# Windowed attention and a top-1 expert layer on one core: two transposing blocks and two couples of pieces a step in place of four single ones

## The chip, the cores and the metric

The kernel runs on one core of a Trainium2 chip. The metric is the device time in microseconds (us) of one execution; of several runs the median is given. A profile is one further execution, recorded by the hardware profiler, with its own time. The engines are named as in the profile: PE (TensorE matmuls; PEld are its weight loads), DVE (VectorE), ACT (ScalarE), POOL (GpSimd) and SP (the queue from which most transfers are issued).

## What is computed

Eight batches of eight heads, 576 rows of 64 columns each, go through causal attention in which a row sees itself and the 63 rows before it. The eight heads side by side make 4608 rows x of 512 columns, and each row goes through one of eight experts.

```
    scores = scale * np.matmul(q, k.transpose(0, 1, 3, 2))
    mask = (rel >= 0) & (rel < window)
...
    attn = np.exp(scores)
    attn = attn / (np.sum(attn, axis=-1, keepdims=True) + 1e-09)
    return np.matmul(attn, v).astype(np.float32)
...
    logits = x @ w_gate + modality_bias[modality_id]
    e_idx = np.argmax(logits, axis=1)
...
        h = np.maximum(x[mask] @ w1[e], 0.0)
        out[mask] = gate_w[mask, None] * (h @ w2[e])
```

w1 is 512 x 1024 and w2 1024 x 512 for each expert. The gate weight is the router's probability of the chosen expert. Everything is float32.

## The kernel before, in words

**Two streams of work.** The 576 rows of a batch are cut into blocks of 64; 72 blocks make 36 pairs (`NPR`). The loop at line 1023 has steps s = 0 to 39, and each step carries several pairs at several stages of attention: the scores of pair s, the probabilities of pair s - 1, the values of pair s - 2, the router's logits of pair s - 3. A group is two pairs, and there are 18 groups (`NG`). In odd steps the rows of group R = (s - 5) // 2 get their ranks within their experts (`route2`, `counts`, `route3`, lines 734 to 796) and are then scattered by POOL into a scratch tensor in HBM that is sorted by expert. From step 12 on (`FIRST`), the expert layer's work on rows that lie there already is mixed into the same steps.

**Slots and pieces.** A slot is 256 rows of one expert. Its products are split into a high and a low part (three float32r matmuls for one product) and dealt out in 16 pieces by a generator, `slot_pieces` (line 268); each call of `gap(it, True)` (line 462) puts the next piece on PE. `first` (line 292) is 12 matmuls of 256 columns into the bank `em`; two of them make 256 columns of the hidden layer, which ACT (`hh`, line 312) and DVE (`hl`, line 313) then copy out. `second` (line 316) is 6 matmuls of 512 columns into `y0` or `y1`, which DVE scales (line 334) and POOL scatters to the output (line 337). What a piece leaves for the other engines is kept in `later` and issued at the next `run_later()`. From step 13 on there are four pieces in a step: in three steps of four, two of `first` and then two of `second`; in the fourth (16, 20, 24 and so on) `second`, `first`, `first`, `second`.

**What a step of attention puts on PE.** `values` (32 small matmuls, line 668), `logits` (line 697), `scores` (line 612), then `probs_t` twice: four transposes of 128 x 128 into a bank, which ACT copies to `pT` (line 647). Below, p0 and p1 are these two groups of four. Then exps on ACT (line 638, eight a pair, in parts of two, three and three), `x_t` (four transposes of the attention's rows, copied by ACT to `xaT`, line 689, which the next step's logits read), and, up to step 33, two parts of `heads_t` (line 566): four transposes each of loaded q or k rows of group G = s // 2 + 1, copied to `kT` or `qT` by `heads_out` (line 575). Even steps take k (`PARTS[0]`: K0, K1), odd steps q. The copies are DVE's, except K1's, which is ACT's.

**Banks.** All these transposes, the logits and the ranks write to PSUM banks of 512 float32 a partition, which `turn_bank` (line 514) hands out. Up to step 11 it takes turns among five banks. From step 13 on it hands out the two banks `tp` of `ps_t` alone (line 474), and who asks for a bank waits until its last reader is through.

**What sets the order.** The order on every engine is that of the program (line 869, `manual_schedule`). PE, ACT and DVE each work through their queue in that order. Small DVE work that isn't urgent is queued: `routing` holds the steps of `route1` and `route3` (the largest logit, the one-hot row `oh`, its running sum, the target row, the scatter), `queue` the planner's. `tick(n)` (line 129) issues n of them, routing's first. `weights(s)` (line 1011) splits loaded weights into their two parts, on ACT and DVE. `plan` (line 804), at the end of a step, takes the counts of a group and queues what decides the next slot's rows. SP issues all loads in the order of the program: q, k and v at the head of a step, weights in `weights`, a slot's rows in `fetch`.

**A step from 13 on, before the change, by the order on PE:** values, logits, scores, p0, p1; piece 1; x_t; piece 2; the first part of the heads; the ranks (odd steps); piece 3; the second part of the heads; piece 4.

Of the kernel before, what the change touches and what calls it, by code (L numbers as in the profile page):

```python
# [26 lines left out]
def tile_window_attn_moe(  # L27
# [12 lines left out]
    nc = tc.nc  # L40
# [10 lines left out]
    NPR = NBLK // 2  # L51
    GB = 2
    GBLK = 2 * GB
    NG = NPR // GB
# [9 lines left out]
    EARLY = ((2, (0, 1)), (4, (0, 1)), (6, (0, 1)), (8, (0, 1)), (9, (1, 2)), (10, (1, 2)), (11, (1, 2)),  # L64
             (12, (0, 2)), (13, (0, 2)), (15, (0, 2)))
    WEIGHTS = 5
    FIRST = 12
# [16 lines left out]
    tab = ctx.enter_context(tc.tile_pool(name="tab", bufs=1))  # L84
# [44 lines left out]
    def tick(n=1, table=False):  # L129
        for _ in range(n):  # L130
            if routing and not table:
                routing.pop(0)()
            elif queue:
                queue.pop(0)()
                issued[0] += 1
# [111 lines left out]
    def run_later():  # L247
        while later:
            later.pop(0)()
# [207 lines left out]
    def counted():  # L457
        for _ in slot_pieces():
            position[0] += 1
            yield  # L460

    def gap(it, wait=False):

        if next(it, "end") != "end" and not wait:
            run_later()
            tick()

    def turn(out_, in_, p0=0):
        n = in_.shape[0]
        nc.tensor.transpose(out=out_, in_=in_, identity=ident[p0:p0 + n, p0:p0 + n])  # L470
# [10 lines left out]
    pl = actx.enter_context(tc.tile_pool(name="pl", bufs=2))  # L481
# [11 lines left out]
    def by_group(x):  # L493
        return x.rearrange("p (a h j) i -> p a h j i", a=2, h=HP)
# [19 lines left out]
    def turn_bank(s):  # L514

        i = n_tp[0]
        n_tp[0] += 1
        if s < FIRST and i % 5 > 1:
            return ps_m.tile([P, 512], F32, name=("em", "y0", "y1")[i % 5 - 2])
        return ps_t.tile([P, 512], F32, name="tp")  # L520
# [13 lines left out]
    def swap_v(p):  # L534

        nc.gpsimd.tensor_copy(out=ve[p][0:W64], in_=vo[p][0:W64])
# [29 lines left out]
    def heads_t(G, nm, i, tp):  # L566


        src = qk[G, nm].rearrange("p t (h a) d -> p t h (a d)", a=2)
        for h in range(2):  # L570
            for t in range(2):
                n = 2 * h + t
                turn(tp[:, n * P:(n + 1) * P], src[:, t, 2 * i + h])

    def heads_out(tp, G, nm, i, copy):
        dst = by_group(qT if nm == "q" else kT)[:, G % 2, 2 * i:2 * i + 2]
        copy(out=dst.rearrange("p h j (i t) -> p h t (j i)", t=2),
             in_=tp.rearrange("p (h t i) -> p h t i", h=2, t=2))
# [54 lines left out]
    def exps(p, us):  # L633
        ss, mn, sm = st[p, "s"]
        for u in us:
            a, hp = divmod(u, HP)
            h = 2 * hp + a
            nc.scalar.activation(  # L638
                out=ss[a][:, hp, :], in_=ss[a][:, hp, :], func=AF.Exp,
                bias=mn[:, h:h + 1], scale=-1.0, accum_out=sm[:, h:h + 1])  # L640
# [43 lines left out]
    def x_t(p, xp):  # L684
        xa = st[p, "xa"]
        for c in range(NC1):
            turn(xp[:, c * P:(c + 1) * P], xa[:, c * P:(c + 1) * P])
        xaT = st[p, "xT"] = work.tile([P, DM], F32, name="xaT")
        nc.scalar.copy(out=xaT, in_=xp)
# [44 lines left out]
    def route2(G, tp):  # L734

        while routing:
            routing.pop(0)()
        oh = chosen[G]
        rk = tp[:, 0:GB * E]
        nc.tensor.matmul(  # L740
            out=rk, lhsT=tri, rhs=oh[:, 1:].rearrange("p j e -> p (j e)"), start=True, stop=False)
        for j in range(GB):
            sh = [P, GB - j, E]
            nc.tensor.matmul(
                out=rk[:, j * E:], lhsT=ones, rhs=oh[:, j:j + 1, :].broadcast_to(sh),
                start=False, stop=(j == GB - 1))
        return rk
# [43 lines left out]
    def counts(G, tp):  # L791
        cp = tp[:, GB * E:E + GB * E]
        nc.tensor.matmul(out=cp, lhsT=ones, rhs=chosen[G + 1][:, 0, :], start=True, stop=True)
        return cp

    def counts_out(pool, cp):
        cnt = pool.tile([1, E], F32, name="cnt")
        nc.vector.tensor_copy(out=cnt, in_=cp[0:1])
        return cnt
# [68 lines left out]
    it = counted()  # L868
# [142 lines left out]
    def weights(s):  # L1011

        if halves:
            split_lo(*halves.pop(0))
        if len(raws) == 2 or raws and not pieces:
            split_hi(*raws[0])
            halves.append(raws.pop(0))
        while pieces and len(raws) < 2:
            x, c = pieces.pop(0)
            raw = epool.tile([P, WCH], F32, name="y", bufs=4)  # L1020
            raws.append((load_piece(raw, evs[x], c), x, c))

    for s in range(NPR + 4):
        j = s % GB
        for f, args in at.pop(s, ()):
            f(*args)
        n_tick = 6 if s < FIRST else 5
        n_gap = 0 if s < FIRST else 4
        G = s // GB + 1
        heads = PARTS[j] if G < NG else ()  # L1030
        R = (s - 5) // GB if s >= 5 and j == 1 else -1
        if 1 <= s < FIRST:
            swap_upper(s - 1)

        if 2 <= s < NPR + 2:
            values(s - 2)
            if s <= FIRST:
                values_out(s - 2)
        if 3 <= s < NPR + 3:
            logits(s - 3, turn_bank(s) if s != FIRST else ps_m.tile([P, 512], F32, name="y0"))  # L1040
            if (s - 3) % GB == GB - 1:
                route1((s - 3) // GB)
        if FIRST < s < NPR + 2:
            values_out(s - 2)
        if s < NPR:
            scores(s)
            if s == FIRST:
                x_turn(fetched[0])
                gap(it, True)
            minima(s)  # L1050
            if s == FIRST - 2:
                tick(todo[0][-1] - issued[0], table=True)
        if 1 <= s <= NPR:
            if s == FIRST:
                run_later()
            if s >= FIRST:
                swap_upper(s - 1)
            swap_v(s - 1)
            for a in range(2):
                probs_t(s - 1, a, turn_bank(s))  # L1060
            sums(s - 1)
        if s < NPR:
            exps(s, (0, 1))
        if s == 0:
            first_pair(1, (both[:1], both[1:]))
            cast_bias()
        if n_gap > 0 and s != FIRST:
            gap(it, True)
        if 2 <= s < NPR + 2:
            x_t(s - 2, turn_bank(s) if s != FIRST else ps_m.tile([P, 512], F32, name="y0"))  # L1070
        run_later()
        tick(2)
        if s < NPR:
            exps(s, (2, 3, 4))
        if n_gap > 0:
            if FIRST < s < FIRST + 4 or s % 2:
                weights(s)
            if s != FIRST:
                gap(it, True)
        if heads:  # L1080
            tp = turn_bank(s)
            heads_t(G, *heads[0], tp)
            heads_out(tp, G, *heads[0], nc.vector.tensor_copy)
        if s == FIRST:
            weights(s)
            gap(it, True)
        run_later()
        tick(n_tick)
        cnt = None
        if R >= 0:  # L1090
            tp = turn_bank(s)
            rk = route2(R, tp)
            if R == NG - 1 or any(R == T for T, _ in EARLY):
                cnt = counts_out(tab if R == NG - 1 else pl, counts(R, tp))
            route3(R, rk)
        if s < NPR:
            exps(s, (5, 6, 7))
        if n_gap > 2:
            if FIRST <= s < FIRST + 4:
                weights(s)  # L1100
            gap(it, True)
        if heads:
            tp = turn_bank(s)
            heads_t(G, *heads[1], tp)
            heads_out(tp, G, *heads[1], nc.scalar.copy if heads[1] == K1 else nc.vector.tensor_copy)
        run_later()
        tick(n_tick)
        if s == WEIGHTS:
            load_weights()
        if s >= WEIGHTS:  # L1110
            weights(s)
        if n_gap > 3:
            gap(it, True)
        run_later()
        if s == 1:
            select_bias()
        if s == 4:
            nc.sync.dma_start(out=xs_blk[DUMMY:DUMMY + 2].rearrange("b p c -> p b c"), in_=padrow)
        for T, xs_ in EARLY:
            if T == R:  # L1120
                plan(T, xs_, cnt)
# [20 lines left out]
    tab = Room()  # L1142
# [99 lines left out]
    while next(it, "end") != "end":  # L1242
# [6 lines left out]
        for n in range(RAWS):  # L1249
            if n < len(swaps) and n == len(ahead) and swaps[n][0] <= t + RAWS:  # L1250
                _, buf, x, c = swaps[n]
# [18 lines left out]
    with tc.If(trip > 0):  # L1270
        NS = N // P + E
        with ExitStack() as gctx:
# [38 lines left out]
            with tc.For_i(0, trip, 1) as it:  # L1311
# [25 lines left out]
                for n in range(F // 512):  # L1337
                    tp = gps.tile([P, 512], F32, name="gxp")
# [53 lines left out]
```

## Time and profile before

| | |
|---|---|
| median of 3 runs | 622.42 us (621.82 to 624.05) |
| the profiled execution | 621.29 us |
| its span, from the first to the last instruction | 619.6 us |
| PE busy | 603.5 us (97%), 6365 matmuls |
| PE weight loads | 542.2 us (88%) |
| DVE busy | 381.8 us (62%), 1486 instructions |
| ACT busy | 297.4 us (48%), 933 instructions |
| POOL busy | 139.7 us (23%), 315 instructions |
| mean granted TensorE clock | 0.992 |
| from HBM and to HBM | 67.49 MB and 23.91 MB |

A row of the timeline reads: start and length in us, the engine, the line of the kernel, the operation, output <- inputs by the program's names, shapes, and how many alike were merged into the row; in brackets how long the engine stood idle before it and who released it. A row of a group of instructions gives, after the bar, the busy time in us and the mean of one in ns, and after a second bar the idle time ahead of them. Matmuls overlap, and their ends are modelled, so their spacing is read from one start to the next. Step 14 begins at 95.13 us, step 16 at 116.21, step 18 at 138.23, step 19 at 148.71, and step 33 ends at 307.15, by the first `values` matmul of a step.

### The profile page before, as it was taken

Reading aid. Unit: us, or ns where it says so; the run is one execution under the profiler, and the core shown is the slowest. Engines: PE = TensorE matmul, PEld = TensorE weight load, DVE = VectorE, ACT = ScalarE, POOL = GpSimd, SP = SyncE. Lnnn points to the kernel's source line nnn. Section 1 sums busy time; section 2 is a strip of 40 time slices with the busy share of each in tenths; the row PEclk is TensorE's granted clock in tenths of the full one; section 3 lists DMA queues with packets and bytes.
Section 4 is the critical chain, followed back from the end, with each engine's and each line's share of the span. In section 5 each row is a group of like instructions: output and inputs, shape, how many; then the busy total and the mean of one; then the engine's idle time right before and its main releaser. Section 6 shows DMA issues by size and latency. Waiting matters only on the chain. (4 is left out here: it accounts for less than half of the span.)

```text
span 619.6 us, 17314 instructions
## 1 busy us (share of the span) xinstructions
PE 603.5 (97%) x6365; PEld 542.2 (88%) x6365; DVE 381.8 (62%) x1486; ACT 297.4 (48%) x933; POOL 139.7 (23%) x315
## 2 busy tenths in 40 slices
PE   8999889999999999999999999999999999999996
PEld 5888778889898998989898899999999989999986
DVE  3899987877776877667656465323324734776622
ACT  3999886765757555636463111111112513554411
POOL 6333422042313320321223131011001101102202
PEclk7999999999999999999999999999999999999999
DMA  9999865764675754463313034522243534678300
GB/s 163 216 234 246 204 183 166 188 188 126 167 205 123 194 135 99 137 155 84 107 54 103 35 103 167 174 69 69 51 155 116 167 126 137 203 239 249 108 18 21
DMA packets 158983, 88.08 MB, mean 142 GB/s; under 512 B 122618, under 2 KB 141616, under 8 KB 158768
## 3 DMA queue, kind: packets, MB, share of 16 engines
q1 hardware_dynamic: 150272, 67.45, 43.1%
q0 software_dynamic: 5888, 18.93, 8.1%
q8 instruction: 51, 0.84, 0.6%
q10 hardware_dynamic: 2736, 0.58, 0.5%
q14 instruction: 36, 0.29, 0.2%
HBM read 67.49 MB, written 23.91 MB: 148 GB/s over the span
## 5 line engine op out<-in xcount | busy, mean ns | idle before, releaser
L326 PE MATMUL y<-Whi,hh 128*128 128x512 f32 x288 | 116.9, 406 | 0.0
L638 ACT ACTIVATE ss<-ss,mn 128x128 f32<-128x128 f32 x288 | 112.6, 398 | 4.0 <-DMA wg<-in_moe_w_gate_dram 3.3
L326 PE MATMUL y<-Wlo,hh 128*128 128x512 f32 x288 | 112.7, 391 | 0.0
L326 PE MATMUL y<-Whi,hl 128*128 128x512 f32 x288 | 112.5, 391 | 0.0
L337 POOL DMA_INDIRECT out_dram<-y,id x36 | 39.8, 1107 | 232.7 <-DVE y L334 159.9
L313 DVE SCALAR_TENSOR_TENSOR hl<-em,hh 128x512 fp32r<-128x512 f32 x50 | 34.5, 690 | 92.8 <-ACT hh L312 82.1
L304 PE MATMUL em<-xh,Whi 128*128 128x256 f32 x400 | 83.7, 290 | 0.0
L312 ACT ACTIVATE hh<-em 128x512 fp32r<-128x512 f32 x50 | 29.6, 592 | 105.2 <-PE em L304 86.9
L304 PE MATMUL em<-xl,Whi 128*128 128x256 f32 x400 | 79.3, 280 | 0.0
L304 PE MATMUL em<-xh,Wlo 128*128 128x256 f32 x400 | 79.1, 279 | 0.0
L647 ACT COPY pT<-tp 128x512 f32<-128x512 f32 x57 | 31.4, 589 | 70.2 <-PE tp L470 60.9
L626 DVE CUSTOM_DVE_ANT_0 ss<-sp,masks 128x128 f32<-128x128 f32 x288 | 63.5, 286 | 2.4 <-PE sp L612 2.3
L326 PEld LDWEIGHTS y<-Whi,hl 128*128 128x128 f32 x288 | 54.1, 188 | 12.2
L304 PEld LDWEIGHTS em<-xh,Whi 128*128 128x128 f32 x400 | 62.3, 189 | 1.8
L326 PEld LDWEIGHTS y<-Whi,hh 128*128 128x128 f32 x288 | 54.2, 188 | 8.2
L326 PEld LDWEIGHTS y<-Wlo,hh 128*128 128x128 f32 x288 | 54.2, 188 | 7.9
L304 PEld LDWEIGHTS em<-xl,Whi 128*128 128x128 f32 x400 | 60.9, 188 | 0.0
L304 PEld LDWEIGHTS em<-xh,Wlo 128*128 128x128 f32 x400 | 60.9, 188 | 0.0
L638 ACT ACTIVATION_READ_ACCUMULATOR ss<-ss,mn 128x1 f32 x288 | 56.0, 195 | 0.0
L773 POOL DMA_INDIRECT xs_scratch<-xa,idx x36 | 36.4, 1012 | 81.8 <-DVE lm L716 40.3
L312 ACT ACTIVATE hh<-sp 128x512 fp32r<-128x512 f32 x22 | 13.2, 598 | 75.9 <-PE sp L304 73.9
L668 PEld LDWEIGHTS av<-ve,pT 128*64 128x64 f32 x576 | 36.3, 138 | 13.2 <-issue 8.2
(240 smaller groups left out, 1211.3 us busy)
## 6 DMA issues: line engine op xcount, KB each, us to landing
xt<-xs_scratch SPq DMA_DIRECT2D x72, 128.0 KB
vo<-in_v_dram SPq DMA_DIRECT2D x32, 256.0 KB
y<-in_moe_w_dram SPq DMA_DIRECT2D x32, 256.0 KB
vo<-in_moe_w_dram SPq DMA_DIRECT2D x24, 256.0 KB
ss<-in_moe_w_dram SPq DMA_DIRECT2D x24, 256.0 KB
xs_scratch<-xs_scratch SPq DMA_DIRECT2D x8, 514.0 KB
pT<-in_moe_w_dram SPq DMA_DIRECT2D x16, 256.0 KB
qk<-in_k_dram SPq DMA_DIRECT2D x14, 256.0 KB
```

What stands on the lines that cost most here:

```text
L304: nc.tensor.matmul(out=hb[:, i * TP:(i + 1) * TP], lhsT=w[buf][:, c0:c0 + P], rhs=x[:, c * TP:(c + 1) * TP], start=(n == 0), stop=(n == le ...
L312: nc.scalar.activation(out=hh, in_=hb, func=AF.Relu),
L313: nc.vector.scalar_tensor_tensor(out=hl, in0=hb, scalar=0.0, in1=hh.bitcast(F32), op0=ALU.max, op1=ALU.subtract)))
L326: nc.tensor.matmul(out=sl["y", t], lhsT=h[:, i * TP + t * P:i * TP + (t + 1) * P], rhs=w[buf][:, c0:c0 + DM], start=(k == 0 and n == 0), s ...
L337: ins = nc.gpsimd.indirect_dma_start(out=out, out_offset=bass.IndirectOffsetOnAxis(ap=sl["id"][:, t:t + 1], axis=0), in_=y, in_offset=None ...
L626: nc.vector.tensor_tensor_reduce(out=ss[a][:, hp, :], in0=sp[a][:, hp * P:(hp + 1) * P], in1=mask, scale=-1.0 / 8.0, scalar=3.0e38, op0=AL ...
L638: nc.scalar.activation(out=ss[a][:, hp, :], in_=ss[a][:, hp, :], func=AF.Exp, bias=mn[:, h:h + 1], scale=-1.0, accum_out=sm[:, h:h + 1])
L647: nc.scalar.copy(out=pT, in_=pp)
L668: nc.tensor.matmul(out=by_block(av)[c * W64:(c + 1) * W64, a, :, hp, :], lhsT=pT[:, i:i + W64], rhs=(vo if c else ve)[p][:, 2 * hp + a, :] ...
L773: ins = nc.gpsimd.indirect_dma_start(out=xs, out_offset=bass.IndirectOffsetOnAxis(ap=idx[:, j:j + 1], axis=0), in_=xg[j], in_offset=None)
```

## The change

From step 13 on, the transposing work of a step stands in two blocks in place of four. The ranks of an odd step are put at its very beginning, ahead of `values`. The first part of the heads follows the probabilities, ahead of piece 1. Pieces 1 and 2 follow each other, with the evictions of piece 1, three ticks, three exps and `weights` issued between them. `x_t` and the second part of the heads follow piece 2, then two ticks, five ticks, the last three exps, and pieces 3 and 4. The exps 2 to 4 stay behind piece 1; the exps 5 to 7 stay ahead of piece 3, now behind the copies of x_t and of the second part. `plan` stays at the end of the step. Up to step 12 the order is as it was. The order on PE from step 13 on becomes: ranks (odd steps), values, logits, scores, p0, p1, first part of the heads; pieces 1 and 2; x_t, second part of the heads; pieces 3 and 4.

The diff:

```diff
@@ -1029,6 +1029,26 @@
         G = s // GB + 1
         heads = PARTS[j] if G < NG else ()
         R = (s - 5) // GB if s >= 5 and j == 1 else -1
+
+        def part(i):
+            if not heads:
+                return
+            tp = turn_bank(s)
+            heads_t(G, *heads[i], tp)
+            heads_out(tp, G, *heads[i], nc.scalar.copy if heads[i] == K1 else nc.vector.tensor_copy)
+
+        def ranks():
+            tp = turn_bank(s)
+            rk = route2(R, tp)
+            n = None
+            if R == NG - 1 or any(R == T for T, _ in EARLY):
+                n = counts_out(tab if R == NG - 1 else pl, counts(R, tp))
+            route3(R, rk)
+            return n
+
+        cnt = None
+        if s > FIRST and R >= 0:
+            cnt = ranks()
         if 1 <= s < FIRST:
             swap_upper(s - 1)
 
@@ -1064,45 +1084,41 @@
         if s == 0:
             first_pair(1, (both[:1], both[1:]))
             cast_bias()
-        if n_gap > 0 and s != FIRST:
+        if s > FIRST:
+            part(0)
+            gap(it, True)
+            run_later()
+            tick(3)
+            if s < NPR:
+                exps(s, (2, 3, 4))
+            if s < FIRST + 4 or s % 2:
+                weights(s)
             gap(it, True)
         if 2 <= s < NPR + 2:
             x_t(s - 2, turn_bank(s) if s != FIRST else ps_m.tile([P, 512], F32, name="y0"))
+        if s > FIRST:
+            part(1)
         run_later()
         tick(2)
-        if s < NPR:
+        if s < NPR and s <= FIRST:
             exps(s, (2, 3, 4))
-        if n_gap > 0:
-            if FIRST < s < FIRST + 4 or s % 2:
-                weights(s)
-            if s != FIRST:
-                gap(it, True)
-        if heads:
-            tp = turn_bank(s)
-            heads_t(G, *heads[0], tp)
-            heads_out(tp, G, *heads[0], nc.vector.tensor_copy)
+        if s <= FIRST:
+            part(0)
         if s == FIRST:
             weights(s)
             gap(it, True)
         run_later()
         tick(n_tick)
-        cnt = None
-        if R >= 0:
-            tp = turn_bank(s)
-            rk = route2(R, tp)
-            if R == NG - 1 or any(R == T for T, _ in EARLY):
-                cnt = counts_out(tab if R == NG - 1 else pl, counts(R, tp))
-            route3(R, rk)
+        if s <= FIRST and R >= 0:
+            cnt = ranks()
         if s < NPR:
             exps(s, (5, 6, 7))
         if n_gap > 2:
             if FIRST <= s < FIRST + 4:
                 weights(s)
             gap(it, True)
-        if heads:
-            tp = turn_bank(s)
-            heads_t(G, *heads[1], tp)
-            heads_out(tp, G, *heads[1], nc.scalar.copy if heads[1] == K1 else nc.vector.tensor_copy)
+        if s <= FIRST:
+            part(1)
         run_later()
         tick(n_tick)
         if s == WEIGHTS:
```

## The prediction

> **What bounds the kernel now.** I read the page first, then the waits of TensorE, then the busy time by step, then the timeline of single steps.
>
> ```profile
> span 619.6 us, 17314 instructions
> ...
> PE 603.5 (97%) x6365; PEld 542.2 (88%) x6365; DVE 381.8 (62%) x1486; ACT 297.4 (48%) x933; POOL 139.7 (23%) x315
> ...
> PEclk7999999999999999999999999999999999999999
> ...
> L647 ACT COPY pT<-tp 128x512 f32<-128x512 f32 x57 | 31.4, 589 | 70.2 <-PE tp L470 60.9
> ```
>
> PE is busy 97% of the span. A busy PE could still hide stretched matmuls, so I cut the stage that the change touches at the first `values` matmul of each step.
>
> ```profile
> core 0: us, PE busy (x) PEld busy (x) DVE busy (x) ACT busy (x) POOL busy (x), PEclk, DMA share, GB/s
> 0.00:20.00 20.00, 17.13 (x184) 12.47 (x188) 10.29 (x65) 9.57 (x35) 10.09 (x54) 0.83 0.90 169
> ...
> 116.21:127.57 11.36, 10.68 (x138) 9.41 (x137) 8.73 (x40) 7.78 (x26) 2.63 (x5) 1.00 0.59 162
> ...
> 138.23:148.71 10.48, 10.48 (x138) 9.45 (x137) 6.85 (x35) 5.45 (x22) 2.87 (x4) 1.00 0.54 151
> 148.71:159.33 10.62, 10.62 (x141) 9.59 (x140) 7.86 (x32) 7.61 (x25) 1.98 (x6) 1.00 0.69 167
> 95.13:307.15 212.02, 211.34 (x2758) 190.38 (x2757) 154.16 (x715) 128.07 (x450) 54.76 (x110) 1.00 0.58 151
> ```
>
> 95.13 to 307.15 holds steps 14 to 33. PE is idle for 0.68 us of it, all in step 16 (116.21 to 127.57); the other steps follow each other without a hole. So nothing runs beside PE that could absorb a delay: a stop of PE there moves the end by its own length, and the only gain to be had is in PE's own spacing, or in step 16's stop.
>
> **The new order on PE.** Before: front (values, logits, scores, eight transposes of probabilities), piece, x_t, piece, heads[0], ranks, piece, heads[1], piece. After: ranks, front, heads[0], two pieces, x_t, heads[1], two pieces. Ranks and each transposed part hold a `tp` bank of `ps_t`, of which there are two, and from step 13 on nothing else is drawn from. Before, a piece (about 1.4 us) stood ahead of x_t and heads[0], in which the earlier bank was emptied. After, three groups of four transposes (p0, p1 of the probabilities, then heads[0]) stand back to back on two banks: one of them must wait for ACT to copy out p0. The trace shows this wait once, in step 16, and what it consists of:
>
> ```profile
> 118.74 0.65 PE L470 MATMUL tp<-ident_r,ss 128*128 128x128 f32 x4
> ...
> 119.44 0.59 ACT L647 COPY pT<-tp 128x512 f32<-128x512 f32 x1
> ...
> 120.08 0.66 PE L470 MATMUL tp<-ident_r,ss 128*128 128x128 f32 x4 [0.68 <-ACT pT L647]
> ...
> 120.49 0.48 PE L326 MATMUL y<-Whi,hh 128*128 128x512 f32 x1
> ```
>
> p1 waits there for ACT's copy of p0: copy ends 119.44 + 0.59 = 120.03, PE resumes at 120.08, 0.05 later. Now the undisturbed pace, from three groups on different banks, and the copies of an even step (18), an odd one (19), step 13 and one late case (29):
>
> ```profile
> 26.36 0.66 PE L470 MATMUL em<-ident_r,ss 128*128 128x128 f32 x4
> 26.86 0.60 PE L470 MATMUL y<-ident_r,ss 128*128 128x128 f32 x4
> 27.29 0.60 PE L470 MATMUL y<-ident_r,xa 128*128 128x128 f32 x4
> ...
> 140.76 1.09 PE L470 MATMUL tp<-ident_r,ss 128*128 128x128 f32 x8
> ...
> 141.46 1.07 ACT L647 COPY pT<-tp 128x512 f32<-128x512 f32 x2 [3.90 <-PE tp L470]
> ...
> 151.24 1.09 PE L470 MATMUL tp<-ident_r,ss 128*128 128x128 f32 x8
> ...
> 151.99 1.08 ACT L647 COPY pT<-tp 128x512 f32<-128x512 f32 x2 [2.26 <-PE tp L470]
> ...
> 86.38 0.66 PE L470 MATMUL tp<-ident_r,ss 128*128 128x128 f32 x4
> ...
> 87.44 0.66 PE L470 MATMUL tp<-ident_r,ss 128*128 128x128 f32 x4 [0.41 <-DVE lg L702]
> ...
> 256.82 1.09 PE L470 MATMUL tp<-ident_r,ss 128*128 128x128 f32 x8
> ...
> 258.13 0.59 ACT L647 COPY pT<-tp 128x512 f32<-128x512 f32 x1 [3.75 <-PE tp L470]
> ```
>
> A third group is ready 27.29 - 26.36 = 0.93 us after p0 begins. In an even step ACT's copy of p0 begins 0.70 after p0 and takes 0.589, so the bank is free to PE at 0.70 + 0.59 + 0.05 = 1.34: PE stops 0.41. The first group after a stop takes 0.50 (26.36 to 26.86), a following one 0.43: another 0.07. Together 0.48. In an odd step the copy begins 0.75 after p0: 0.53. ACT cannot begin earlier, since it starts as soon as p0 has landed. Behind the waiting transposes stand both pieces of the first couple, and nothing of PE can pass them.
>
> heads[0] exists in steps 13 to 33, 21 steps. In step 13 p1 is already held up to 1.06 after p0 by DVE's logits, so heads[0] would come at 1.06 + 0.50 = 1.56, after p0's bank is free. In step 16 p1 sits in p0's bank, and heads[0] finds the other one empty. Both keep their old stops and get no new one. The rest: 10 odd x 0.53 + 9 even x 0.48 = **+9.6 us**.
>
> **What the joining saves.** Step 18 before and rows in which a couple runs unbroken:
>
> ```profile
> 141.61 0.48 PE L304 MATMUL em<-xh,Whi 128*128 128x256 f32 x2
> ...
> 143.12 0.60 PE L470 MATMUL tp<-ident_r,xa 128*128 128x128 f32 x4
> 143.47 0.48 PE L304 MATMUL em<-xh,Whi 128*128 128x256 f32 x2
> ...
> 330.86 0.37 PE L304 MATMUL em<-xh,Whi 128*128 128x256 f32 x1
> ...
> 333.75 0.40 PE L326 MATMUL y<-Whi,hh 128*128 128x512 f32 x1
> ...
> 323.44 0.18 PE L740 MATMUL tp<-oh,tri 128*128 128x16 bf16 x1
> ...
> 323.55 0.48 PE L326 MATMUL y<-Whi,hh 128*128 128x512 f32 x1
> ...
> 326.46 0.27 PE L668 MATMUL av<-ve,pT 128*64 128x64 f32 x1
> ```
>
> Before, from the first piece to the step's end: 148.71 - 141.61 = 7.10. After: heads[0] 0.43, the first couple 333.75 - 330.86 = 2.89, x_t and heads[1] 0.35 (143.12 to 143.47) + 0.43 = 0.78, the second couple 326.46 - 323.55 = 2.91: 7.01. It saves 0.09 a step, 21 x 0.09 = **-1.9**. A switch between transposes and pieces is thus nearly free, and halving their number is worth little. In steps 34 to 37 x_t only changes its neighbours: nothing.
>
> **Ranks first.** In an odd step they cost 10.62 - 10.48 = 0.14 (0.11 of it between 323.44 and 323.55). Between a piece and `values` no row shows them: from 0, if they vanish in the spacing there, to 0.28, twice the present cost, if PE's pipeline restarts on both sides of them. I take 0.14 again, the nearest row: nothing, with -2 to +2 us over 14 steps for the range. DVE's add of the ranks (and a copy of the counts) waits for them at the head of the step; queued behind it on DVE are the logits' add, on which p1's bank hangs, values_out and the minima. PE reaches p1 some 2.9 us later (front), enough for two adds of under 0.2. The scatters' index work and their two POOL transfers come half a step earlier, ahead of the next step's `swap_v` and `sums`; these are needed a step later, and POOL is busy 23%. SP's transfers keep their order; those that wait for scattered rows can only be released earlier.
>
> **The other moves.** exps 5 to 7 now follow x_t's copy, heads[1]'s copy and the relu on ACT (48% busy), with a couple and the front between them and their reader: nothing. heads[1]'s eviction comes earlier than before. heads[0] wants its q/k rows some 3 us earlier in the step:
>
> ```profile
> 153.75 2.10 SPq L563 DMA_DIRECT2D qk<-in_k_dram  x4
> ```
>
> The k rows for step 20 are issued by 155.85, the new heads[0] comes near 159.33 + 3.4 = 162.7: 6.9 us for them to land. Nothing, unless SP falls back by more than half of that.
>
> **Sum.** 9.6 - 1.9 = +7.7. The profiled execution took 621.29 (1.7 around its span) and becomes 629.0; the median of the runs shown, 622.42, becomes **630.1 us**.
>
> **Rivals.** (1) *The dearer bank.* The program puts p1 into p0's bank in most steps, as in step 16, now that DVE reaches the logits later. The stop is then 120.49 - 118.74 = 1.75 against 141.61 - 140.76 = 0.85: 0.90 a step, 19 x 0.90 - 1.9 = +15.2, 637.6. A late copy as in step 29 (1.31 after p0) would cost the like: 1.31 + 0.59 + 0.05 - 0.93 + 0.07 = 1.09. For it: step 16; against: no other step between 95 and 307 has it. Chance 0.20.
>
> (2) *No stop, the other side.* heads[0]'s bank is empty in time, and only the joining counts: -1.9, 620.5; if the stops of steps 13 (0.56) and 16 (0.90) go too, -3.4, 619.0. It decides if the copy of p0 ends less than 0.93 after p0 begins. Against it: 1.29 and 1.34 in the rows. The Trainium skill, Perfetto Trace Analysis, section Matmuls, says that independent groups should rotate through PSUM banks so that one's evacuation overlaps the next one's matmuls; by that, alternating two banks would give this rival's time. The rows of step 16 speak against it for groups as short as 0.43 us beside a copy of 0.59. Chance 0.09.
>
> (3) *Ranks wait.* In step 18 the one-hot rows were ready well before use:
>
> ```profile
> 146.21 0.68 DVE L313 SCALAR_TENSOR_TENSOR hl<-em,hh 128x512 fp32r<-128x512 f32 x1
> ...
> 147.75 0.17 DVE L724 TENSOR_TENSOR oh<-wn,wm 128x16 bf16<-128x16 f32 x1
> ```
>
> Afterwards hl waits for ACT's x_t copy, heads[1] copy and relu, some 0.6 each, which begin 0.7 after x_t at about 145.4; hl ends near 148.4, oh near 148.8, and the ranks want it at about 149.1. If this chain slips by over 0.3, PE stops at the head of 6 to 13 odd steps, by some 0.5: +3.0 to +6.5 more, 633.1 to 636.6. Chance 0.08.
>
> (4) *The clock.* The stops break PE's activity, and the granted clock falls, as it stood at 0.83 in the first 20 us. Over 212 us that is 212 x (1/0.83 - 1) = 43, 673.5 with the rest. The row of step 16 holds a stop of 0.68 and a clock of 1.00. The Trainium skill, TensorE: Matmul & The Clock Gate, section A second HAM failure mode: psum-queue depth-cycling, reports a clock that swings where matmuls cycle through PSUM banks with short idles; the trace does not agree for single stops of this size. Chance 0.02.
>
> **How the numbers follow.** The forecast has what is left, 0.61. A measurement here can tell about 0.5%, 3.1 us, from no change. Its case, (1), (3) and (4) are slower by more than that: 0.90. Of (2), 0.03 is faster and 0.06 the same, and 0.01 of the forecast ends within 3.1 us: 0.07 the same. The range reaches from 625.5 (the forecast less 2 for the ranks and less a quarter of the stops) to 638.5, past (1); left out are (2), (4) and the far end of (1).
>
> **What would show it.** In the changed profile, steps 14, 15 and 17 to 33 hold a stop ahead of the first transposes of qk, released by ACT's pT, of about 0.4; steps are 10.9 to 11.0 long; the couple of 24 matmuls takes 2.9; ranks start without idle time; PEclk stays at 9. Wrong would be steps of 10.4 without a stop (2), p1 stopped in place of heads[0] (1), or idle time ahead of L740 (3).

## The result, and the profile after

After takes 639.39 us (median of 4 runs, 638.92 to 639.92), before 622.12 (4 runs, 621.03 to 624.05). The ratio is 1.0274, with a 95% interval from 1.0247 to 1.0302: 2.7% slower. The forecast was 630.1. The direction was right; the loss is 17.3 us where 7.7 were forecast.

The lines of the page of after that answer to those of before:

```profile
span 637.7 us, 17296 instructions
...
PE 610.3 (96%) x6365; PEld 543.2 (85%) x6365; DVE 381.4 (60%) x1486; ACT 296.3 (46%) x933; POOL 140.3 (22%) x315
...
PEclk9999999999999999999999999999999999999999
...
L337 POOL DMA_INDIRECT out_dram<-y,id x36 | 40.0, 1110 | 221.8 <-DVE y L334 158.8
...
L773 POOL DMA_INDIRECT xs_scratch<-xa,idx x36 | 39.3, 1093 | 150.2 <-DVE Wlo L119 71.4
L647 ACT COPY pT<-tp 128x512 f32<-128x512 f32 x57 | 31.1, 589 | 78.3 <-PE tp L470 77.4
```

The work is the same on every engine, and the span is 18.1 us longer. The row to notice is L773, the scatters. On the page of before it reads:

```profile
L773 POOL DMA_INDIRECT xs_scratch<-xa,idx x36 | 36.4, 1012 | 81.8 <-DVE lm L716 40.3
```

Before, one took 1012 ns, and the largest share of the idle time ahead of it was ended by `lm` of line 716. Now one takes 1093 ns, and it is `Wlo`, the weights' low part, that ends the wait. The scatters have come to another place.

The busy time by stretch, cut as in the prediction at the first `values` matmul: steps 14 to 33, step 18, step 19.

```profile
core 0: us, PE busy (x) PEld busy (x) DVE busy (x) ACT busy (x) POOL busy (x), PEclk, DMA share, GB/s
95.44:324.38 228.94, 218.14 (x2758) 192.17 (x2757) 153.97 (x711) 127.52 (x451) 55.76 (x111) 1.00 0.54 140
141.29:153.17 11.88, 11.30 (x141) 9.80 (x140) 5.71 (x31) 6.33 (x23) 3.82 (x7) 1.00 0.38 109
153.17:164.11 10.94, 10.65 (x140) 9.45 (x137) 8.84 (x39) 6.39 (x23) 0.19 (x1) 1.00 0.66 159
```

Steps 14 to 33 went from 212.02 to 228.94 us, and PE, idle for 0.68 there before, is now idle for 10.80. Step 19 lost 0.32 (10.62 to 10.94), step 18 lost 1.40 (10.48 to 11.88). Two different things have happened.

Step 19 shows the forecast stop. The rows are of its probabilities' transposes and of the first part of the heads:

```profile
155.70 1.09 PE L470 MATMUL tp<-ident_r,ss 128*128 128x128 f32 x8
157.09 0.66 PE L470 MATMUL tp<-ident_r,qk 128*128 128x128 f32 x4 [0.29 <-ACT pT L647]
```

heads[0] starts 1.39 after p0; in the prediction's three rows on free banks the third group comes at 0.93. The waits of PE name ACT's `pT` 21 times, 19 of them ahead of heads[0] in steps 13 to 33 (the other two lie in step 12, 2.4 long, and ahead of p1 in step 16):

```profile
engine line waited for: us in total, times, longest us
PE tp L470 <- ACT pT L647: 11.2, 21, 2.4
...
PE tp L470 <- DVE lg L702: 1.4, 3, 0.7
...
PE sp L612 <- issue: 1.1, 4, 0.3
```

Step 18 shows what was not forecast. First the front of step 18 of before, PE, DVE and POOL:

```profile
139.21 0.59 PE L697 MATMUL tp<-wg,xaT 128*64 128x8 f32 x16
139.73 1.10 PE L612 MATMUL sp<-kT,qT 64*64 64x128 f32 x32
...
139.85 0.17 DVE L702 TENSOR_TENSOR lg<-tp,bias_sel 128x8 f32<-128x8 f32 x1 [1.08 <-PE tp L697]
...
144.11 1.07 POOL L773 DMA_INDIRECT xs_scratch<-xa,idx  x1 [6.49 <-DVE lm L716]
...
145.66 0.97 POOL L773 DMA_INDIRECT xs_scratch<-xa,idx  x1 [0.28 <-POOL xa L772]
```

And of after:

```profile
142.27 0.59 PE L697 MATMUL tp<-wg,xaT 128*64 128x8 f32 x16
...
142.71 0.97 POOL L773 DMA_INDIRECT xs_scratch<-xa,idx  x1 [0.28 <-POOL xa L772]
...
142.79 1.00 PE L612 MATMUL sp<-kT,qT 64*64 64x128 f32 x20
...
144.08 0.67 PE L612 MATMUL sp<-kT,qT 64*64 64x128 f32 x12 [0.29 <-issue]
...
144.19 0.17 DVE L702 TENSOR_TENSOR lg<-tp,bias_sel 128x8 f32<-128x8 f32 x1 [3.25 <-PE tp L697]
```

Before, DVE took up the logits 0.05 after they ended (139.80 to 139.85), scores ran through in 1.03 (139.73 to 140.76, the next row in the prediction's fence), and the first scatter began 3.4 us after p0 (140.76 to 144.11), beside pieces. After, a scatter starts while the logits are still running. They end at 142.86, and DVE takes them up at 144.19, 1.33 later, with PE named as the one it waited for. PE itself stops after 20 of 32 scores, for nothing that the profile shows ("issue"), and scores take 1.89.

### The profile page after: what moved, and what is told of

The parts are those of the page before. It is cut to its first block, busy times and chain, and to the rows that moved or that the text cites. A ratio compares the mean times of both kernels' runs of the same rounds, so it can differ in the third digit from the quotient of the medians.

```text
span 637.7 us, 17296 instructions
## 1 busy us (share of the span) xinstructions
PE 610.3 (96%) x6365; PEld 543.2 (85%) x6365; DVE 381.4 (60%) x1486; ACT 296.3 (46%) x933; POOL 140.3 (22%) x315
## 5 line engine op out<-in xcount | busy, mean ns | idle before, releaser
L326 PE MATMUL y<-Whi,hh 128*128 128x512 f32 x288 | 115.1, 400 | 0.0
L304 PE MATMUL em<-xh,Whi 128*128 128x256 f32 x400 | 82.3, 287 | 0.0
L773 POOL DMA_INDIRECT xs_scratch<-xa,idx x36 | 39.3, 1093 | 150.2 <-DVE Wlo L119 71.4
L612 PE MATMUL sp<-kT,qT 64*64 64x128 f32 x1152 | 44.2, 277 | 3.0 <-issue 1.1
```

The lines of the kernel that those rows point to most:

```text
L304: nc.tensor.matmul(out=hb[:, i * TP:(i + 1) * TP], lhsT=w[buf][:, c0:c0 + P], rhs=x[:, c * TP:(c + 1) * TP], start=(n == 0), stop=(n == le ...
L326: nc.tensor.matmul(out=sl["y", t], lhsT=h[:, i * TP + t * P:i * TP + (t + 1) * P], rhs=w[buf][:, c0:c0 + DM], start=(k == 0 and n == 0), s ...
L612: nc.tensor.matmul(out=sp[a][c * W64:(c + 1) * W64, hp * P:(hp + 1) * P], lhsT=qT[rows, place(g + c, hp), :], rhs=kT[rows, win(c, hp), :], ...
L773: ins = nc.gpsimd.indirect_dma_start(out=xs, out_offset=bass.IndirectOffsetOnAxis(ap=idx[:, j:j + 1], axis=0), in_=xg[j], in_offset=None)
```

## The experiments

Beside the median stands the time of steps 18 to 35, from the first `values` of step 18 to that of step 36. It leaves out steps 12, 13 and 16, which hang in the main on loads (the first slot's rows in step 12, the weights in step 16), and which differ by up to several us between kernels whose code is the same there. For before it is 188.23 us, for after 203.06. The ratios are taken to runs of before from the same time: their median is 622.12 for after, 622.30 for hold, av, av_hold and before_ranks, 622.06 for the first four dummy kernels, and 622.31 for the rest.

| kernel | median us | ratio to before, 95% | steps 18 to 35, us | against before |
|---|---|---|---|---|
| after | 639.39 | 1.0274 (1.0247 to 1.0302) | 203.06 | +14.83 |
| hold: scatters held back | 633.92 | 1.0181 (1.0158 to 1.0204) | 196.95 | +8.72 |
| av: third bank for heads[0] | 631.02 | 1.0143 (1.0110 to 1.0176) | 193.81 | +5.58 |
| av_hold: both | 625.80 | 1.0049 (1.0030 to 1.0067) | 188.91 | +0.68 |
| av_hold16: both, step 16 as in after | 623.95 | 1.0028 (1.0012 to 1.0044) | 189.39 | +1.16 |
| late_ranks: after, ranks at the old place | 637.47 | 1.0244 (1.0220 to 1.0268) | 200.59 | +12.36 |
| before_ranks: before, ranks first | 623.29 | 1.0017 (0.9999 to 1.0036) | 188.38 | +0.15 |
| before_ranks_hold: that, scatters held back | 621.61 | 0.9986 (0.9971 to 1.0001) | 187.84 | -0.39 |
| dummy_ind: before, 22 indirect DMAs in fronts | 638.67 | 1.0264 (1.0227 to 1.0300) | 197.47 | +9.24 |
| dummy_small: the same, 32 bytes a row | 635.61 | 1.0218 (1.0185 to 1.0251) | 197.28 | +9.05 |
| dummy_direct: the same, direct DMAs | 625.98 | 1.0058 (1.0040 to 1.0076) | 188.16 | -0.07 |
| dummy_copies: copies instead of DMAs | 626.44 | 1.0084 (1.0052 to 1.0117) | 188.37 | +0.14 |
| dummy_under: indirect DMAs under pieces | 626.48 | 1.0057 (1.0038 to 1.0077) | 188.16 | -0.07 |

My theory (theory 1): the loss is the bank stop, about 10 us, and fronts that lie beside a scatter, about 9, less the gain of the joins. The rival (R1): all of it comes from the banks and from ranks in front, on PE, DVE and ACT themselves.

### Holding the scatters back (hold)

```diff
-        routing.append(rows)
+        if s > FIRST:
+            held.append(rows)
+        else:
+            routing.append(rows)
...
             gap(it, True)
             run_later()
+            if j == 0 and held:
+                held.pop(0)()
             tick(3)
```

> After, with one thing put back: the list entry that makes the row numbers and issues the two scatters of a couple (line 773) is run behind the first couple of pieces of the even step, as it was before, instead of in the odd step. The bank stop of heads[0] stays. Theory 1 (of the 17 us lost, about 10 are the bank stop and about 9 are fronts that lie beside a scatter): the scatters lie under pieces again, the fronts of even steps 14 to 34 fall back to about 3.9 us, the ones of odd steps 17, 21, 25, 29, 33 (which lie beside a DMA_INDIRECT of the output) stay stretched, time 630 to 632 us. Rival R1 (all of the loss comes from the banks and from ranks in front, on PE, DVE and ACT themselves): 638 to 640 us, even fronts still 4.1 to 5.1 us long.

Measured: 633.92, 5.5 less than after. Steps 18 and 19 of hold:

```profile
142.47:153.49 11.02, 10.72 (x140) 9.59 (x139) 5.86 (x32) 6.32 (x23) 3.10 (x5) 1.00 0.56 160
153.49:164.44 10.95, 10.66 (x141) 9.46 (x137) 8.85 (x39) 6.40 (x23) 1.50 (x5) 1.00 0.68 172
```

Step 18 falls from 11.88 to 11.02, step 19 stays. From the first matmul of `values` to the first of heads[0], every even front from 18 to 32 takes 3.92 now, as the quiet odd ones do; in after they took 4.11 to 5.10. R1, which left them stretched, has failed. The total missed my 630 to 632 by 2 us.

### Another bank for the first part of the heads (av)

```diff
-            tp = turn_bank(s)
+            tp = ps_a.tile([P, 512], F32, name="av") if i == 0 and s > FIRST else turn_bank(s)
             heads_t(G, *heads[i], tp)
```

> After, with one thing changed: heads[0] of a step from 13 on is put out into the bank named av (free since values_out) instead of into p0's, so that it need not wait for the copy of p0; the scatters stay where after has them. Theory 1: the 0.5 us between p0's end and heads[0] goes, clean odd steps (15, 19, 23, 27, 31) shrink from 10.95 to about 10.45 us, the fronts beside a scatter stay stretched; time 629 to 631 us. Rival R1 (all the loss is the bank): 619 to 622 us. A third view, that the stop only moves to the next user of the banks, the piece or the transposes of x: 637 to 639 us.

Measured: 631.02, 8.4 less than after, and the clean odd steps take 10.43 to 10.45. The rows of step 19, PE and ACT:

```profile
155.81 1.09 PE L470 MATMUL tp<-ident_r,ss 128*128 128x128 f32 x8
...
156.74 0.60 PE L470 MATMUL av<-ident_r,qk 128*128 128x128 f32 x4
```

heads[0] follows p0 after 0.93, the pace that the prediction read for three groups on three banks. ACT's copies run from 156.56 to 157.63, and nobody waits for them. The Trainium skill, Perfetto Trace Analysis, section Matmuls, asks for independent groups to rotate through banks; the pair of kernels agrees, with the addition that two banks were too few for three groups.

### Both repairs, and step 16 (av_hold, av_hold16)

The edits of the two kernels above together; in av_hold16 the bank `av` is left out in step 16 (`and s != 16`).

> Both edits of the two kernels before it at once. Theory 1: neither stop nor stretched even fronts; what is left of the change is the joined couples (-2 us) and what the odd fronts beside an output's DMA_INDIRECT cost in both kernels; 619 to 622 us, so 0 to 0.5% faster than before (622.1). Rival R1: as the kernel with the other bank alone. If the two costs overlap (both hide in the same wait), the sum of the two single gains is larger than the gain of both together.

> The kernel with both repairs (heads[0] in the bank av, scatters held back), but in step 16, where av is read late by values_out's division, heads[0] takes p0's bank as in after. Expected: step 16 back from 14.35 to about 11.5 us, no lowered clock behind it; 622.5 to 624 us, so that the change with both repairs ends where before stands (622.1): the joined couples' gain goes to p0's later turn and the fronts beside the output's DMA_INDIRECT.

Measured: 625.80 and 623.95. In steps 18 to 35 the two single edits save 6.11 and 9.25, together 14.15, not far from their sum, 15.36: in the main they repair two different things. av_hold misses the 619 to 622 expected. What I overlooked is step 16, 14.35 us long: p1 waits 1.15 for the copy of p0 there, heads[0] waits 0.63 more until DVE's `values_out` has read the bank `av`, and behind the two stops the granted clock halves. Two stretches of av_hold's step 16:

```profile
122.00:124.00 2.00, 1.37 (x10) 1.00 (x9) 1.97 (x14) 1.35 (x5) 0.00 (x0) 0.96 0.77 171
124.00:126.00 2.00, 2.00 (x7) 1.61 (x6) 1.77 (x9) 0.12 (x2) 0.00 (x0) 0.50 0.31 70
```

With p0's bank in that step it takes 11.48, as expected. Neither version beats before: freed of both costs, the new order is still 0.28% slower (1.0012 to 1.0044).

### Ranks first, alone and undone (before_ranks, late_ranks, before_ranks_hold)

before_ranks is before with `ranks()` at the head of the odd step; late_ranks is after with it behind x_t and heads[1] of the odd step, ahead of the second couple:

```diff
-        if s > FIRST and R >= 0:
-            cnt = ranks()
...
-        if s <= FIRST and R >= 0:
+        if R >= 0:
             cnt = ranks()
```

> Before, with the second part of the change alone: ranks (route2, route3) come first in the odd step instead of behind its third couple of pieces. heads and couples stay. Its scatters are then due in the tick behind the first pieces of the odd step, so theory 1 expects them under pieces, not in a front: 620 to 623 us, within 0.5% of before. If ranks in front is dear in itself (it waits on DVE's one-hot), 627 us or more. If the scatters run into the next step's front here too, fronts of even steps longer than 3.5 us and 626 to 631 us.

> After with the second part of the change undone: ranks (route2, route3) stand behind the second couples of the odd step again, heads and joined couples stay. Theory 1 (ranks in front cost nothing themselves, but they bring the scatters forward into the even fronts): as the kernel that only holds the scatters back, 632 to 635 us, even fronts 3.92. If ranks in front were a gain or a loss of more than 2 us by themselves, it differs from 633.9 by that.

> Before with ranks first and the scatters held back to the place that they have in before: the second part of the change without its side effect. Theory 1: even fronts 3.39 in all steps, steps 14, 16, 30 and 34 lose what they had in the kernel with ranks first alone (0.4 to 0.9 us each); 620.5 to 622 us, at most 0.3% under before.

before_ranks: 623.29, within 0.5% of before, but not for the reason that I gave. Its scatters do reach the front; of the eleven even fronts from 14 to 34 four have stretched scores (1.37 to 1.72), in steps 14, 16, 30 and 34, and in four others POOL paid instead. POOL and PE in step 20 of before_ranks:

```profile
161.98 2.69 POOL L773 DMA_INDIRECT xs_scratch<-xa,idx  x1 [12.33 <-DVE qT L577]
...
162.54 1.10 PE L612 MATMUL sp<-kT,qT 64*64 64x128 f32 x32
163.58 1.09 PE L470 MATMUL tp<-ident_r,ss 128*128 128x128 f32 x8
```

The scatter takes 2.69 in place of 1.07, and scores keep their 1.03. With the scatters held back (before_ranks_hold) all even fronts from 14 to 34 are 3.38 or 3.39 but step 16's, which is 4.28 as in before; at 621.61 against 622.31 the interval still touches 1.

late_ranks I got wrong: 637.47, where 632 to 635 was expected. Its even fronts are 3.92 as expected, but the clean odd steps take 11.54 to 11.58 in place of 10.95. PE's waits in late_ranks say why:

```profile
PE tp L470 <- ACT pT L647: 9.6, 20, 1.9
PE tp L740 <- ACT xaT L689: 3.2, 11, 0.3
```

Behind x_t and heads[1] the ranks are a third group on two banks again, and wait for ACT's copy of x_t. So in the new order, ranks in front save 3.6 us in steps 18 to 35 (200.59 to 196.95, with scatters out of the front in both), and the scatters that come with them cost 6.1 (196.95 to 203.06).

### Scatters that do nothing but issue (the five dummy kernels)

These are before with added work that nothing reads. The edit of dummy_ind, behind the last piece of the odd steps 13 to 33:

```diff
+        if FIRST <= s < 34 and j == 1:
+            nc.vector.tensor_copy(out=mark[:, 0:1], in_=idc[0:1, 0:1])
+            for _ in range(2):
+                nc.gpsimd.tensor_copy(out=mark[:, 1:2], in_=mark[:, 0:1])
+                nc.gpsimd.indirect_dma_start(
+                    out=extra.pop(), out_offset=bass.IndirectOffsetOnAxis(ap=place_i, axis=0),
+                    in_=masks.rearrange("p m c -> p (m c)"), in_offset=None)
```

dummy_small sends `[:, 0:8]` of the rows; dummy_direct calls `dma_start(out=extra.pop(), in_=...)`; dummy_copies makes five POOL copies of 128x16 instead; dummy_under has dummy_ind's lines behind the second piece of the odd step, ahead of heads[0].

> Before, unchanged in its order, with added work: at the end of the odd steps 13 to 33, behind the last piece, POOL copies one word and issues an indirect DMA of 128 rows of 1536 bytes to a scratch tensor that nothing reads, twice, so that 22 DMA_INDIRECT lie in the 11 fronts of the even steps 14 to 34, where after has its scatters. No bank, no rank and no couple is moved. Theory 1 (the DMA_INDIRECT in the front holds back PE's semaphore updates and stretches values, scores or p0): 11 times 0.3 to 0.9, time 625 to 632 us, PE's updates up to 1 us late there. R1 (banks and ranks alone): 621 to 623 us, fronts 3.39 as in before.

> The same with added indirect DMAs of 32 bytes a row instead of 1536 (1/48 of the bytes, as many rows). If it is the bytes and what they take from other transfers: no more than 1 us over before. If it is the issuing of 128 rows by POOL: as the kernel with the long rows, within 2 us.

> The same with added direct DMAs from POOL's queue of the same 196 KB each to the same place. If only the indexed form does it: 621 to 623 us. If every DMA that POOL issues does it: 625 us or more, with PE's updates late in the direct issue too.

> The control: at the same places two times six short POOL copies, about as long as two DMA_INDIRECT, and no DMA. Theory 1: 621 to 623 us, fronts 3.4 us, none of PE's updates late there. If any work of POOL in the front (its delayed swap of values and sums) does it: as the kernel with the indirect DMAs.

> The 22 added indirect DMAs of 1536 bytes a row once more in before, with one thing changed: they are released in the middle of the odd steps 13 to 33, behind their second couple of pieces, so that they run beside the 128x512 and 128x256 matmuls of the pieces and not beside the front. Theory 1 (it is the meeting of a DMA_INDIRECT with the small matmuls of the front that costs): steps 14 to 34 as in before, within 0.1 us each; 622 to 627 us (the kernels with added copies and direct DMAs, whose steps 14 to 36 are those of before, stood at 626). If a DMA_INDIRECT costs wherever it lies: 632 to 639 us, as with the ones in the front.

By their totals four of the five miss what was expected: dummy_ind lies above 625 to 632, dummy_small 3.1 under dummy_ind where 2 was allowed, and dummy_direct and dummy_copies stand at 626, above 621 to 623. In their profiles all five lose 2.1 to 5.0 us in steps 12 and 13 together, all of it in step 12, ahead of the first added transfer, and up to 1.5 in steps 16 and 17; that is why the totals of the three controls stand at 626. The traces show what holds step 12 up. In all five DVE waits there for the first slot's rows (`xt`, 1.2 to 3.4 us; in before it does not), ACT's `xh` and its copy of the transposes to `pT` follow late, and PE waits for that copy, 3.1 to 5.4 us where before waits 1.85. In dummy_under:

```profile
81.24 1.30 DVE L267 STREAM_TRANSPOSE xt<-xt 128x512 f32<-128x512 f32 x2 [3.34 <-DMA xt<-xs_scratch]
...
84.25 1.12 PE L471 MATMUL tp<-ident_r,Whi 128*128 128x128 f32 x4 [5.29 <-ACT pT L648]
```

Why the rows land later stays open. The stretch from step 18 to 35 is clear of it, and the readings below rest on it. Its rows in dummy_ind, dummy_direct and dummy_under, one fence each:

```profile
145.68:343.15 197.47, 193.31 (x2467) 171.34 (x2466) 130.60 (x631) 109.85 (x397) 71.16 (x137) 1.00 0.58 145
```

```profile
144.81:332.97 188.16, 188.16 (x2467) 169.71 (x2466) 131.26 (x631) 110.24 (x396) 63.38 (x137) 1.00 0.60 153
```

```profile
145.64:333.80 188.16, 188.16 (x2467) 169.71 (x2466) 131.43 (x630) 110.63 (x396) 67.10 (x130) 1.00 0.61 151
```

With no bank, rank or couple moved, indirect DMAs in the even fronts cost 9.2 us and open holes in PE (193.31 busy of 197.47). Seven of the nine even steps from 18 to 34 pay, 0.8 to 1.6 each; in steps 20 and 24 the added DMAs begin 3.09 after `values`, behind the start of p1, and these two steps are as in before. Rows of 32 bytes cost as much (9.05) as rows of 1536, so it is not the bytes. Direct DMAs from POOL at the same place, POOL copies, and the same indirect DMAs beside pieces cost nothing. It takes both: the indexed form, and the front (in dummy_under the DMAs also ran beside heads[0] or the ranks in most steps, at no cost). Step 18 of dummy_ind, PE and POOL:

```profile
146.67 1.07 POOL L1123 DMA_INDIRECT extra<-masks,place_i  x1 [0.16 <-issue]
...
147.18 1.19 PE L613 MATMUL sp<-kT,qT 64*64 64x128 f32 x22
...
148.65 0.41 PE L613 MATMUL sp<-kT,qT 64*64 64x128 f32 x3 [0.28 <-issue]
...
149.37 0.48 PE L613 MATMUL sp<-kT,qT 64*64 64x128 f32 x7 [0.31 <-issue]
149.78 1.09 PE L471 MATMUL tp<-ident_r,ss 128*128 128x128 f32 x8
```

It is the picture of after without its change: scores cut into three, 2.60 in place of 1.03.

## Why the prediction was too low

**The bound** was read rightly: PE without a hole, so that every stop is paid in full.

**The bank stop** was forecast as 0.48 in even and 0.53 in odd steps, 9.6 in all. A front without a scatter went from 3.39 to 3.92, 0.53 in even steps too (ACT's copy starts 0.75 after p0 there as well); 19 steps make 10.1. Step 16 got no new stop, as said. In step 13 the prediction was wrong: p1 no longer waits for the logits (it starts 0.49 after p0, in before 1.07), so heads[0] pays the bank stop there too; the step as a whole is 0.34 shorter (11.29 to 10.95), and it lies outside the sum below. The third bank, which takes the stop away, gives back 8.4 of the total: shown.

**Joining** was forecast to save 1.9. Taking the terms below from the 18.05 us that steps 14 to 36 grew by leaves -1.7 for it and all small moves. The couples of step 19 take 2.89 and 2.92, where 2.89 and 2.91 were read. No kernel has the joining alone, so the term stands only as that remainder. av_hold, which has it together with ranks in front and neither of the two costs, fits the forecast in size: its four clean pairs of steps (18 and 19, 22 and 23, 26 and 27, 30 and 31) are 0.08 to 0.17 shorter than those of before, where 0.18 a pair was forecast.

**Ranks first** is the step that failed. The prediction put "nothing, with -2 to +2 us" on it, and of what comes with it: "The scatters' index work and their two POOL transfers come half a step earlier, ahead of the next step's `swap_v` and `sums`; these are needed a step later, and POOL is busy 23%." It asked who waits for POOL, and how full POOL is; it did not ask what runs on PE while they issue. In after the two scatters of a group fall into the even front. The excess of the eleven even fronts over 3.92 (4.42 in step 16, 3.38 in step 34, which hold has there) is 6.6 us; holding the scatters back gives 5.5 of the total, and 6.1 of steps 18 to 35, whose even fronts hold 6.0 of the 6.6: shown. Nor are ranks in front nothing by themselves: in the new order they save 3.6 us, which the prediction did not see, since it looked at the ranks and at the banks apart.

**DVE's queue in odd steps** was judged to have room for "two adds of under 0.2" ahead of the logits' add. In steps 17 and 25, behind the fourth kind of step, the eviction of `second` (0.75) stands there as well. DVE and PE in step 17:

```profile
131.87 0.75 DVE L334 TENSOR_SCALAR y<-y,gate 128x512 f32<-128x512 f32 x1
132.54 0.14 DVE L798 COPY cnt<-tp 1x8 f32<-1x8 f32 x1
132.61 0.15 DVE L754 TENSOR_TENSOR tgt<-tp,ebase 128x16 f32<-128x16 f32 x1
132.69 0.14 DVE L702 TENSOR_TENSOR lg<-tp,bias_sel 128x8 f32<-128x8 f32 x1
...
132.91 1.06 PE L470 MATMUL tp<-ident_r,ss 128*128 128x128 f32 x8 [0.69 <-DVE lg L702]
```

p0 waits there 0.69 for `lg`; the two fronts lose 0.7 and 0.4. In step 36 PE waits 0.38 for `lg` too, with or without the scatters held back: the step takes 9.23 in after and in hold, 8.76 in before. In steps 21, 29 and 33 p0's copy is late by 0.3 to 0.6, in all 1.5. There a scatter of the output (line 337) begins 2.00 to 2.47 after `values`, beside the probabilities, and PE's semaphore updates of p0 come 0.30 to 0.64 late; no run moved this scatter alone, so that it is the cause is read from the traces. In before the copy was as late in steps 29 and 33 (the prediction quotes 1.31 after p0 for step 29), but there nobody waited for it; now heads[0] does. That is the late copy of rival (1), in three steps of nineteen.

The terms: 10.1 + 0.1 (step 16) + 6.6 + 1.1 + 0.4 (step 36) + 1.5 - 1.7 = 18.1, which is the difference of the two profiled executions (639.43 - 621.29). The last term is the remainder, so the sum closes by construction; the first, and the third, the scatters, are confirmed by av and hold; the terms of DVE's queue and of the output's scatter are read from the traces.

**The rivals.** (1) would have given 637.6, near the truth, by another way: p1 did not move into p0's bank. (2) is what av shows for its clean odd steps, 10.43 to 10.45. (3) did not come: a rank starts 0.18 ahead of `values` in step 17 without a wait. (4) is real in small: with the stop of 2.41 in step 12 the clock is 0.50 from 80 to 82 us of after, and it is so behind step 16 of av_hold; single stops of 0.5 did not lower it (1.00 over 95.44 to 324.38). The Trainium skill, TensorE: Matmul & The Clock Gate, section A second HAM failure mode: psum-queue depth-cycling, reports for another kernel a clock that swings because PE idles shortly but often between groups that cycle through banks. The stops of steps 14 to 33 did not do that here.

## What to carry to other kernels

Of a step that is moved, ask of every transfer that it issues beside which work of the other engines it will now run, not only how busy its own engine is. Count the groups that stand back to back on PE against the banks that they share: three groups of 0.43 us on two banks cost 0.53 us each time in the front, and in late_ranks, where the ranks became the third group behind x_t and heads[1], PE stopped there too. When a change of order moves several things, undo each by itself: here one part (ranks first) hid its own gain behind its side effect.

## What was unexpected of the hardware

**An indirect DMA of POOL and a dense run of small matmuls hold each other up.** Of the even fronts from 14 to 34 of after, av, before_ranks, dummy_ind and dummy_small in which a DMA_INDIRECT of 128 rows began 0.1 to 1.5 us after `values`, those where it took its usual 0.96 to 1.07 us had their scores stretched from 1.03 to 1.37 to 2.64; those where it took about 1.3 had 1.34 to 1.54; and four in before_ranks, where it took 2.0 to 2.7, had 1.03. Among the even fronts of before, hold, av_hold and before_ranks_hold there is none. What is late is what PE tells the others: matched with the ends of instructions, the trace's semaphore updates of ACT and DVE come within 0.02 us everywhere, PE's about 0.014 after the end in the quiet (at most 0.08 in before and after where no DMA_INDIRECT runs within 1 us), and up to 1.37 late in after when the instruction ends while a DMA_INDIRECT runs (41 of 73 by over 0.1; in before 17 of 48). Beside the added DMAs of dummy_ind 25 of 32 are late by over 0.1, up to 2.21; beside the direct DMAs of dummy_direct none of 35, beside the copies of dummy_copies none of 56, and under the pieces of dummy_under one of 14, by 0.22. A DMA_INDIRECT that began at 2.18, behind the scores' start, left scores alone but made step 28 of dummy_ind 0.83 longer by a late copy; one at 3.09, past the start of p1 (step 20), cost nothing.

**It is the issue, not the transfer.** 32 bytes a row cost as much as 1536, and the issue takes 1.017 and 1.016 us. The Trainium skill, Perfetto Trace Analysis, section DMA Instruction — SWDGE (GPSIMD), says that the recorded span of such an instruction ends when its descriptors are made, not when the data have been moved; the equal spans agree. The Trainium skill, DMA: Bandwidth & Descriptors, section SWDGE vs HWDGE vs iDMA, gives direct and indirect DMAs of GpSimd the same software path; here the direct ones (0.61 us each) cost PE nothing at the same place. What PE and the indexed issue share stays open.

**A stop of one to two and a half microseconds lowers the clock only at times.** It stood at 0.50 for 3.4 us behind step 16 of av_hold, with its stops of 1.15 and 0.63, and as long in step 12 of after (one stop of 2.41). It stayed at 1.00 behind the stop of 1.85 in step 12 of before and that of 2.09 in step 16 of dummy_under. What decides it stays open.
